# Issuing most output stores from ScalarE's DMA queue in a fused agent-attention and maxout kernel

## The chip, the cores and the metric

The kernel runs on one core of a Trainium2 chip. The metric is the device time of one execution in microseconds (us). The engines are called as in the profile: PE (matrix products; PEld is its loading of weights), ACT (ScalarE), DVE (VectorE), POOL (GpSimd) and SP (SyncE, which here only issues DMAs). A DMA is issued by an instruction on an engine's queue and then carried out by the 16 DMA engines of the core.

## What is computed

Four batches of 12544 rows of 128 numbers go through agent attention with 49 agents, and the result, 50176 rows, through a maxout layer:

```
a2k     = softmax(scale * agents @ k^T)          # per batch, 49 x 12544
agent_v = a2k @ v                                 # 49 x 128
q2a     = softmax(scale * q @ agents^T)           # 12544 x 49
x       = q2a @ agent_v                           # 50176 x 128 over all batches
h       = max(x @ w1, x @ w2, x @ w3)             # 50176 x 768
out     = h @ w_out                               # 50176 x 128
```

All inputs and the output are float32.

## The kernel before

The 50176 output rows are cut into 49 groups of 1024 rows (8 tiles of 128): 48 groups of one batch each, and group 48, which gathers the last two tiles of every batch. A group `s` of this kind is loaded (`ql.s`, L513, SP), cast to bf16 (`qc.s`, L517, POOL), turned either by a DMA transpose (`qd.s`, L454, SP) or on PE (`qt`, `qe`), and scored against the agents (`sc`, `ex`). The two softmaxes are not divided out at once: the weights w1, w2, w3 are multiplied by the agents' values ahead (the G tiles), so that the hidden layer of a group is a product of G with the group's exponentials (`u` and `v`, L558, PE). Maxout is done as relu of a difference and a maximum: for five of the six hidden blocks ACT makes a relu (`a`, L571, tile AS) and DVE takes the maximum (`x`, L574, tile R); for the block 4 ACT does both (L565 and L568). The products with w_out gather in OM (`li`, L582, and `p`, L592, PE), and DVE scales each half of a group's result into the output tile OS (`ov.s.0`, `ov.s.1`, L599). The store `st.s` (L607) sends OS, 512 KB, to the output in DRAM; group 48 is stored in four pieces of 128 KB.

The keys and values of batch 0 are worked through first (to about 45 us). Those of batches 1 to 3 are worked through beside the groups of the batch before: `kl`, `vl` (L325, loads on SP), `kc`, `vc` (L335, casts on POOL), `kt` (L454, DMA transposes on SP), `ks`, `kx`, `kv`, `va` on PE, ACT, PE and DVE, and the sums of exponentials `ea` on POOL (L474).

Two things set the order. The string `ORDER` names every operation in one list that was written ahead from costs and times; each engine runs its own operations in the order of that list, and each operation waits for the data it needs. In the same list the number behind a slash names the buffer that an operation writes. There are three PSUM tiles for the hidden products (UV), two small ones (OM), thirteen load tiles (LD), thirteen R tiles and nine output tiles (OS). All loads, DMA transposes and stores are on SP, so a DMA that waits there holds every later DMA. The only DMA issued elsewhere is the load of the agents at the very start, on ACT.

The layer that builds the program gives every DMA one of eight completion semaphores in turn, in the order of the list and over all issuing engines. A DMA waits, beside its data and its buffer, for the DMA that had its semaphore before, which is the one eight places earlier in the list. ACT's instructions carry one wait themselves; further waits are put into a semaphore instruction ahead.

```
def dma(kb):
    return dict(cost=(0.45, 1.0), serve=kb / 415.0)
...
SLOTS = {"UV": 3, "OM": 2, "LD": 13, ..., "R": 13, "RC": 4, "OS": 9, ...}
...
add(f"st.{s}", SP, em.store(s), after=[f"ov.{s}.0", f"ov.{s}.1"], use=[f"os.{s}"], cost=(0.45, 1.6), serve=524 / 415.0)
```

Of the kernel before, what the change touches and what calls it, by code (L numbers as in the profile page):

```python
# [260 lines left out]
class Emit:  # L261
# [342 lines left out]
    def store(self, s):  # L604
        def fn():
            for cut, r, n in self.rows(s):
                self.nc.sync.dma_start(self.io["out"][r, :].rearrange("(p j) c -> p j c", j=n), self.t[f"os.{s}"][:, cut, :])  # L607
        return fn


# [176 lines left out]
u.35.3/2 v.35.4 a.35.3/2 re.36/0 p.34.0.2 p.34.0.0 li.34.1/0 qd.43/0 qc.40/2 ov.34.0/0 v.35.3/1 x.35.4/8 u.35.1/2 x.35.3/0  # L787
p.34.1.3 p.34.1.5 a.35.1/1 v.35.5/0 p.34.1.4 ql.44/4 x.35.5/2 u.35.2/1 v.35.1/2 a.35.2/2 p.34.1.1 li.35.0/1 p.35.0.3 x.35.1/4
u.35.0/0 v.35.2/1 a.35.0/0 p.35.0.4 p.35.0.5 x.35.2/5 u.36.5/2 p.34.1.0 a.36.5/1 p.34.1.2 u.36.3/0 ov.34.1 v.35.0/1 a.36.3/2
p.35.0.2 x.35.0/6 st.34 u.36.4/2 sc.37/0 ql.42/8 a.36.4 v.36.5/0 qd.40/1 u.36.1/1 x.36.5/7 p.35.0.0 a.36.1/0 p.35.0.1 v.36.4  # L790
ov.35.0/1 v.36.3/0 x.36.4/3 u.36.0/1 x.36.3/9 qc.44/1 li.35.1/1 p.35.1.5 a.36.0/1 v.36.1/2 p.35.1.2 x.36.1/2 u.36.2/0 ex.37/2
v.36.0/1 p.35.1.3 a.36.2/2 p.35.1.4 x.36.0/5 u.37.3/2 su.37/0 p.35.1.0 a.37.3/0 p.35.1.1 u.37.5/0 re.37/2 ov.35.1 v.36.2/1
a.37.5/1 u.37.4/2 qc.42/2 x.36.2/4 li.36.0/0 p.36.0.0 p.36.0.4 a.37.4 p.36.0.5 u.37.1/0 v.37.5/1 a.37.1/2 v.37.4 x.37.5/6 p.36.0.1
# [23 lines left out]
p.42.1.1 p.42.1.0 u.44.4/0 ov.42.1 v.45.2/2 a.44.4 u.44.5/1 x.45.2/4 p.43.0.5 p.43.0.3 p.43.0.4 a.44.5/2 p.43.0.0 su.44/0 v.44.4  # L817
re.44/1 v.44.5/2 ov.43.0/8 x.44.4/8 u.45.1/1 li.43.1/0 x.44.5/5 p.43.1.3 p.43.1.5 a.45.1/0 v.45.0/0 sc.46/1 x.45.0/0 u.44.3/2
ex.46/3 v.45.1/1 p.43.1.4 a.44.3/2 p.43.1.2 x.45.1/7 u.46.0/0 su.45/1 p.43.1.1 a.46.0/1 p.43.1.0 u.46.2/2 re.45/0 ov.43.1 v.44.3/1
a.46.2/0 u.45.4/0 x.44.3/2 st.43 li.44.0/0 p.44.0.5 st.42 p.44.0.0 a.45.4 p.44.0.2 qd.48/0 u.45.5/2 v.46.2/1 a.45.5/2 v.45.4  # L820
x.46.2/3 p.44.0.4 p.44.0.1 st.37 p.44.0.3 x.45.4/10 sc.47/1 ov.44.0/6 v.46.0/2 u.46.1/1 ex.47/2 v.45.5/0 x.46.0/11 li.45.0/0
a.46.1/0 li.44.1/1 p.45.0.0 p.45.0.4 x.45.5/9 u.45.3/2 v.46.1/1 a.45.3/1 p.44.1.5 p.44.1.2 p.44.1.3 x.46.1/5 u.47.0/0 v.45.3/2
a.47.0/2 p.44.1.1 x.45.3/2 u.47.2/1 p.44.1.4 a.47.2/0 p.44.1.0 u.46.4/0 ov.44.1 v.47.2/2 a.46.4 u.46.5/1 x.47.2/6 su.46/1 p.45.0.2
# [40 lines left out]
```

## Time and profile before

| | |
|---|---|
| median of 3 runs | 446.63 us (446.55 to 449.52) |
| the profiled execution | 448.96 us |
| its span, first to last instruction | 447.1 us |
| mean granted TensorE clock | 0.988 |
| busy: PE, DVE, ACT, POOL | 421.8, 392.1, 393.6, 169.5 us |
| DMA traffic | 121.98 MB, 273 GB/s in the mean |
| SP's DMA queue (q1), share of the 16 engines' time | 90.4% |
| stores on SP | 52 issues (48 of 512 KB, 4 of 128 KB), 5.6 us from issue to landing for the large |
| first store issued | 105.4 us after the start |

The profile shows one execution. A page of it gives each engine's busy time, the span in 40 equal slices (each digit is the busy share in tenths), the DMA queues, and the groups of instructions. Views of the trace give more: waits by engine and by what ended them, the timeline of one engine (start, length, line, tile written and read), busy time in chosen stretches, and all instructions that touch a tile or a line. Issuing a DMA is a row of the engine's queue (`SPq`, `ACTq`) and does not count as busy time. The time from issue to landing is the DMA engines' part.

### The profile page before, as it was taken

How to read it: one execution, taken by the hardware profiler on the slowest of the kernel's cores; microseconds unless marked ns; L12 is line 12 of the kernel's file. 1: busy time of each engine (PE TensorE's matmuls, PEld its weight loads, DVE VectorE, ACT ScalarE, POOL GpSimd, SP SyncE). 2: the span in 40 equal slices, each digit the busy share in tenths (PEclk: the TensorE clock that was granted, in tenths of full speed). 3: DMA queues.
4: the chain of work that ended last, by engine and by line, in shares of the span. 5: the costliest groups of instructions: out<-in, count | busy, mean ns of one | idle time of the engine just before them, and what ended most of it. 6: DMA issues, size and time to landing. Idle time of an engine off the chain costs nothing.

```text
span 447.1 us, 12853 instructions
## 1 busy us (share of the span) xinstructions
PE 421.8 (94%) x5260; PEld 270.8 (61%) x5260; DVE 392.1 (88%) x496; ACT 393.6 (88%) x461; POOL 169.5 (38%) x176
## 2 busy tenths in 40 slices
PE   0787899999999999999899999999999999999996
PEld 0554466666666666666566666666665555655675
DVE  1345799999999999999899999998999999999996
ACT  1469799999999999999889999999999999999983
POOL 1641645555694222824871324527601201000000
PEclk9989699999999999999999999999999999999999
DMA  8999999999999999999999999999699464450405
GB/s 312 410 408 387 346 372 281 298 405 308 327 291 307 352 285 285 345 310 225 321 354 253 313 302 345 303 221 353 189 300 282 103 189 122 90 195 22 164 37 202
DMA packets 97045, 121.98 MB, mean 273 GB/s; under 512 B 70423, under 2 KB 73179, under 8 KB 96987
## 3 DMA queue, kind: packets, MB, share of 16 engines
q1 hardware_dynamic: 96784, 121.07, 90.4%
q8 instruction: 41, 0.67, 0.6%
q14 instruction: 17, 0.14, 0.1%
q10 hardware_dynamic: 203, 0.10, 0.1%
HBM read 78.74 MB, written 25.69 MB: 234 GB/s over the span
## 4 chain that ended last, share of the span: by engine, by line
PE 83%; DMA 8%; DVE 3%; issue 2%; POOL 2%; ACT 1%; SPq 1%; DVEq 0%; POOLq 0%
PE UV L558 35%; PE OM L592 31%; PE OM L582 6%; DMA LD<-in_v_dram 4%; PE OM L533 3%; DVE R L574 2%; PE OM L523 2%; DMA LD<-in_k_dram 2%; PE OM L376 2%; PE OM L359 2%; DMA LD<-in_q_dram 1%; PE OM L545 1%; SPq L325 1%; DVE OS L599 1%; POOL QB L517 1%
## 5 line engine op out<-in xcount | busy, mean ns | idle before, releaser
L574 DVE TENSOR_TENSOR R<-UV,AS 128x1024 bf16<-128x1024 f32 x245 | 293.4, 1219 | 17.8 <-PE UV L558 12.9
L571 ACT ACTIVATE AS<-UV 128x1024 bf16<-128x1024 f32 x245 | 246.3, 1024 | 17.8 <-PE UV L558 13.5
L558 PE MATMUL UV<-EQ,G 49*128 49x512 bf16 (+1 forms) x1248 | 181.7, 371 | 0.9
L592 PE MATMUL OM<-wo_bf,R 128*128 128x128 bf16 x2352 | 180.4, 220 | 0.0
L592 PEld LDWEIGHTS <-R 128*128 128x128 bf16 x2352 | 139.8, 98 | 43.4 <-issue 41.1
L558 PEld LDWEIGHTS <-G 49*128 49x128 bf16 x1248 | 61.5, 94 | 61.8 <-issue 21.7
L517 POOL CAST QB<-LD 128x1024 bf16<-128x1024 f32 x49 | 51.1, 1048 | 98.4 <-DMA LD<-in_q_dram 50.3
L335 POOL CAST KB<-LD 128x1152 bf16<-128x1152 f32 (+2 forms) x45 | 49.7, 1116 | 60.4 <-DMA LD<-in_k_dram 42.8
L599 DVE TENSOR_TENSOR OS<-OM,RC 128x512 f32<-128x512 f32 x98 | 67.1, 684 | 3.6 <-PE OM L592 2.5
L335 POOL CAST VB<-LD 128x1152 bf16<-128x1152 f32 (+1 forms) x33 | 37.3, 1137 | 47.7 <-DMA LD<-in_v_dram 14.7
L565 ACT ACTIVATE UV<-UV 128x1024 f32<-128x1024 f32 x49 | 49.8, 1017 | 2.5 <-PE UV L558 1.2
L568 ACT ACTIVATE R<-UV 128x1024 bf16<-128x1024 f32 x49 | 50.1, 1023 | 1.7 <-PE UV L558 1.2
L582 PE MATMUL OM<-G,EQ 128*128 128x256 bf16 x196 | 37.9, 276 | 0.0
L539 ACT ACTIVATE EQ<-OM 128x512 bf16<-128x512 f32 x49 | 29.5, 602 | 0.9 <-PE OM L533 0.6
L474 POOL TENSOR_TENSOR EA<-EA,EK 128x441 f32<-128x441 f32 x27 | 27.6, 1023 | 4.8 <-ACT EK L365 4.1
L347 DVE COPY KT<-UV 128x1152 bf16<-128x1152 bf16 (+1 forms) x12 | 8.2, 700 | 17.3 <-PE UV L342 17.3
L582 PEld LDWEIGHTS <-EQ 128*128 128x128 bf16 x196 | 12.6, 97 | 15.6 <-issue 14.2
L533 PE MATMUL OM<-QT,agT 128*64 128x512 bf16 (+1 forms) x104 | 20.4, 398 | 0.2 <-DMA QT<-QB 0.2
L365 ACT ACTIVATE EK<-OM 128x441 bf16<-128x441 f32 (+1 forms) x33 | 17.8, 540 | 2.9 <-POOL EA L474 1.6
L376 PE MATMUL OM<-EK,VB 128*128 128x49 bf16 x392 | 17.3, 186 | 2.7 <-ACT VB L333 1.4
L359 PEld LDWEIGHTS <-KT 128*128 128x128 bf16 x392 | 14.6, 98 | 7.5 <-issue 4.5
L376 PEld LDWEIGHTS <-VB 128*128 128x128 bf16 x392 | 14.3, 97 | 7.9 <-issue 5.0
(67 smaller groups left out, 186.1 us busy)
## 6 DMA issues: line engine op xcount, KB each, us to landing
LD<-in_q_dram SPq DMA_DIRECT2D x48, 512.0 KB, 6.4
out_dram<-OS SPq DMA_DIRECT2D x48, 512.0 KB, 5.6
LD<-in_k_dram SPq DMA_DIRECT2D x40, 576.0 KB, 7.3
LD<-in_v_dram SPq DMA_DIRECT2D x40, 576.0 KB, 8.7
LD<-in_k_dram SPq DMA_DIRECT2D x3, 512.0 KB, 9.0
LD<-in_v_dram SPq DMA_DIRECT2D x3, 512.0 KB, 8.1
LD<-in_moe_w_dram SPq DMA_DIRECT2D x6, 192.0 KB, 8.4
KT<-KB SPq DMA_TRANSPOSE x33, 7.0
```

What stands on the lines that cost most here:

```text
L335: (self.nc.gpsimd if eng == POOL else self.nc.vector).tensor_copy(out=out, in_=src)
L376: self.nc.tensor.matmul(out, vb[:, j, :], e[:, j * A:(j + 1) * A], start=False, stop=True, skip_group_check=True)
L517: return lambda: self.nc.gpsimd.tensor_copy(out=self.t[f"qb.{s}"], in_=self.t[f"q.{s}"][:, :GT, :])
L533: self.nc.tensor.matmul(self.t[f"qs.{s}"][h * H:(h + 1) * H, jj * P:(jj + pairs) * P], self.agT[:, b, :], self.t[f"qT.{s}"][:, 2 * jj + h: ...
L558: self.nc.tensor.matmul(t[:, h, jj * P:(jj + pairs) * P], self.t[f"G{b}"][h * H:h * H + A, c + f * P:c + (f + 1) * P], self.t[f"e.{s}"][h ...
L565: return lambda: self.nc.scalar.activation(self.t[f"u.{s}.{f}"], self.t[f"u.{s}.{f}"], AF.Relu)
L568: return lambda: self.nc.scalar.activation(self.t[f"r.{s}.{f}"], self.t[f"u.{s}.{f}"], AF.Relu)
L571: return lambda: self.nc.scalar.activation(self.t[f"a.{s}.{f}"], self.t[f"u.{s}.{f}"], AF.Relu)
L574: return lambda: self.nc.vector.tensor_tensor(out=self.t[f"r.{s}.{f}"], in0=self.t[f"v.{s}.{f}"], in1=self.t[f"a.{s}.{f}"], op=ALU.max)
L582: self.nc.tensor.matmul(self.t[f"o.{s}.{o}"][:, i * 2 * C:(i + 1) * 2 * C], self.t[f"e.{s}"][:, jj * P:(jj + 1) * P], self.t[f"G{of[jj]}"] ...
L592: self.nc.tensor.matmul(self.t[f"o.{s}.{o}"][:, c:c + C], self.t[f"r.{s}.{f}"][:, h, jj * P:(jj + 1) * P], self.wo_bf[:, f, :], start=Fals ...
L599: self.nc.vector.tensor_tensor(out=self.t[f"os.{s}"][:, j:j + 4, :], in0=self.t[f"o.{s}.{o}"].rearrange("p (j c) -> p j c", c=C), in1=self ...
```

## The change

The stores of groups 0 to 45 are issued on ACT's queue; those of groups 46, 47 and 48 stay on SP. In the list, the stores keep their places but for two: `st.34` moves behind `u.36.4 sc.37 ql.42 a.36.4`, and `st.43` behind `li.44.0 p.44.0.5 st.42 p.44.0.0 a.45.4`.

```diff
     def store(self, s):
         def fn():
             for cut, r, n in self.rows(s):
-                self.nc.sync.dma_start(self.io["out"][r, :].rearrange("(p j) c -> p j c", j=n), self.t[f"os.{s}"][:, cut, :])
+                (self.nc.scalar if s < 46 else self.nc.sync).dma_start(self.io["out"][r, :].rearrange("(p j) c -> p j c", j=n), self.t[f"os.{s}"][:, cut, :])
         return fn
...
-p.35.0.2 x.35.0/6 st.34 u.36.4/2 sc.37/0 ql.42/8 a.36.4 v.36.5/0 qd.40/1 u.36.1/1 x.36.5/7 p.35.0.0 a.36.1/0 p.35.0.1 v.36.4
+p.35.0.2 x.35.0/6 u.36.4/2 sc.37/0 ql.42/8 a.36.4 st.34 v.36.5/0 qd.40/1 u.36.1/1 x.36.5/7 p.35.0.0 a.36.1/0 p.35.0.1 v.36.4
...
-a.46.2/0 u.45.4/0 x.44.3/2 st.43 li.44.0/0 p.44.0.5 st.42 p.44.0.0 a.45.4 p.44.0.2 qd.48/0 u.45.5/2 v.46.2/1 a.45.5/2 v.45.4
+a.46.2/0 u.45.4/0 x.44.3/2 li.44.0/0 p.44.0.5 st.42 p.44.0.0 a.45.4 st.43 p.44.0.2 qd.48/0 u.45.5/2 v.46.2/1 a.45.5/2 v.45.4
```

## The prediction

> **What bounds the kernel now.** I read the page's slices first, then busy time by stretch, then the waits of each engine, then the DMA issues line by line, and last the timelines of SP and ACT side by side. All times are of the profiled execution: 448.96 us, of which its span is 447.1; it stands 2.3 us above the median of the runs (446.63), so differences are worked out inside it and added to the median.
>
> The slices show three compute engines full from the fourth slice to the last, and the DMA engines full until slice 30 (about 335 us) and then half idle:
>
> ```profile
> PE   0787899999999999999899999999999999999996
> DVE  1345799999999999999899999998999999999996
> ACT  1469799999999999999889999999999999999983
> DMA  8999999999999999999999999999699464450405
> ```
>
> The stretches say how full (columns: length, then busy us and instructions of PE, PEld, DVE, ACT, POOL, then clock, DMA share, GB/s). ACT has 46 to 48 of 50 us, DVE the same:
>
> ```profile
> 150.00:200.00 50.00, 49.88 (x657) 32.56 (x655) 47.77 (x60) 48.18 (x57) 21.67 (x21) 1.00 1.06 309
> 200.00:250.00 50.00, 48.47 (x617) 31.64 (x616) 46.78 (x59) 46.34 (x55) 26.65 (x28) 1.00 1.10 289
> 335.00:400.00 65.00, 64.60 (x667) 36.78 (x665) 61.75 (x68) 61.23 (x69) 9.11 (x9) 1.00 0.58 158
> ```
>
> Who waits for whom (us in total, times, longest): ACT waits in many small pieces for PE's hidden products; SP waits in long ones, 40.6 us of them at the stores; of the compute engines only POOL, 38% busy, waits long for DMAs.
>
> ```profile
> ACT AS L571 <- PE UV L558: 13.5, 38, 1.0
> ACT EK L365 <- POOL EA L474: 1.6, 1, 1.6
> POOL QB L517 <- DMA LD<-in_q_dram: 50.3, 8, 11.9
> SPq L607 <- DVE OS L599: 40.6, 7, 16.1
> ```
>
> So ACT, DVE and PE bound the kernel together. After 50 us all idle time before ACT's instructions is 24.4 us, and the part of it that goes back to a DMA is the one gap of 1.55 us at 216.57. Whatever holds ACT is nearly all lost; whatever helps SP is worth little.
>
> **Gain.** SP loses 46 of its 52 store issues, at a median of 0.52 us some 24 us of SP's time, and its waits for output tiles:
>
> ```profile
> L607 SPq DMA_DIRECT2D out_dram<-OS x52: 332/518/1336, 105.4 to 444.3; - x52
> L454 SPq DMA_TRANSPOSE KT<-KB x33: 1232/3076/9312, 46.5 to 311.8; - x33
> L454 SPq DMA_TRANSPOSE QT<-QB x27: 1232/1645/5177, 132.2 to 414.7; - x27
> ```
>
> (durations in ns, least/median/most). SP is on the chain of waits for 1%, and the DMA pieces there (8%) lie before 42 us, ahead of the first store at 105.4. The bytes stay the same while the DMA engines are full. DVE's wait for a store to free an output tile is 0.3 us in all. The gain is between 0 and 1.55 + 0.3 = 1.9 us; I take 0, since POOL's delay behind that one gap comes from loads whose DMA engines are as full as before.
>
> The Trainium skill, "DMA: Bandwidth & Descriptors", section "Issuing engines are not separate DMA queues", says that moving a DMA to another engine saves only the issuer's time; the shares above bear that out.
>
> **Cost 1, the issue itself on ACT.** The trace has one ACT issue, 0.57 us, for another shape. Bounds for a store: 0.33 us (least on SP) and 1.34 us (most). I take 0.55. Forty-six of them are 25 us if they lie bare, 0 if the queue part of ACT issues while its datapath computes. The trace says the latter: of 340 semaphore instructions on ACT after 50 us the median ends 0.44 us before the ACTIVATE that it guards starts, while the ACTIVATE before it is running (ACT's large ACTIVATEs follow each other at 0.92 us). So an issue has about 0.44 + 0.92 = 1.3 us in which it costs nothing; 0.55 fits, and two in a row (stores 2 and 5, 25 and 27, 44 and 45) just fit. I take 0.4 us in sum, for stores 41 and 39, issued together at 399.4 just as tile 41 becomes ready. If that lead is gone, the cost is the 25 us.
>
> **Cost 2, what ACT now waits for.** In the built order each store still waits for its tile and for the landing of the DMA that stands eight places before it in the program, because eight completion semaphores are handed round over all DMAs. On ACT both waits hold the ACTIVATEs behind them. The tile: ready 3 to 75 us before ACT reaches the store, except stores 23 (0.78 us), 41, 43 and 34 (the two that the order moves later: 1.46 and 1.63); no cost beyond the above. The eighth DMA before: SP lags ACT by up to 8 us between 165 and 270 us, so here the room is thin. Landing against the start of ACT's next instruction: store 9 212.19 against 210.57, store 7 172.94 against 173.13, store 17 246.22 against 246.32, stores 20, 19, 23 and 33 0.3 to 0.9 us ahead, all others over 1.5 us. With 0.6 us for issue and release, store 7 costs 0.4 us and store 9, once ACT is 0.4 late, 1.8 more; then ACT is late enough for the rest. Sum 2.2 us. Behind each stand ACT's relus, for them wait DVE's max, PE's output products and PE's next hidden products (three UV tiles).
>
> **Cost 3, issues that meet a long issue of SP.** While the DMA engines are full, a transpose keeps SP issuing for up to 9.3 us:
>
> ```profile
> 164.93 1.32 SPq L454 DMA_TRANSPOSE QT<-QB  x1
> 166.29 8.02 SPq L454 DMA_TRANSPOSE KT<-KB  x1
> 174.41 1.00 SPq L325 DMA_DIRECT2D LD<-in_v_dram  x2
> 175.46 0.43 SPq L607 DMA_DIRECT2D out_dram<-OS  x1
> ```
> ```profile
> 167.34 3.05 ACT L571 ACTIVATE AS<-UV 128x1024 bf16<-128x1024 f32 x3
> 170.29 1.02 ACT L565 ACTIVATE UV<-UV 128x1024 f32<-128x1024 f32 x1
> ```
>
> Store 6 now stands on ACT before the instruction at 170.29, in the middle of SP's 8.02 us. Nothing in the trace shows an ACT issue beside a transpose. Lower bound: it is not held, 0. Upper bound: it begins when SP's issue ends, as SP's own did at 175.46. Then the delay is the end of SP's row plus 0.6 us minus the start of ACT's next: store 0 (kt1.8 ends 105.34) 2.4, store 1 (113.17) 2.9, store 6 (174.31) 4.6, store 8 (194.27) 3.9, store 13 (209.57) 1.6, store 19 (267.98) 1.6, store 26 (295.52) 1.6, store 37 (416.86) 1.4; together 20.0, with store 9's wait 22.2. The nearest row is the start, where both engines issue at once: ACT's 98 KB take 0.57 us, and SP's first five loads 0.39 to 0.69 us each, where alone they take 0.33. Each slows the other there, so I lean to sharing. But a delay of 3 us shifts ACT against SP, the later meetings change, and ACT's idle time takes some back: I take half, 11 us, and keep 0 and 25 for the range (25: no meeting lost, ACT twice caught behind the same queue).
>
> The Trainium skill, "Perfetto Trace Analysis", section "DMA Instruction — HWDGE (DVE, Sync)", says that an issue locks the descriptor generator for itself until all its descriptors are made. By that rule it would be all 22.2 us, 469 us; no run so far shows it.
>
> **Sum.** 0 gain + 0.4 + 11 (the 2.2 of cost 2 is in it) = 11.4; 446.63 + 11.4 = 458.0 us.
>
> **Rivals.**
> A, not slower: ACT's issue never waits for SP's. Then 0.4 + 2.2 = 2.6 us: 449.2 us, within 1%. For it: SP's plain loads and stores take about 0.5 us even with eight DMAs in flight, so only a transpose fills anything. Against it: the start's rows. It decides if no ACT issue is over 1.4 us.
> B, the eighth-DMA wait becomes the bound: a store now passes SP's loads that would have gone first. SP's landings follow each other at 1.43 us (165.67, 167.09, 168.52), so each passed load lands that much later; the seven stores with under 1 us of room would cost 1.4 us more each at worst, of which ACT's own lateness spares about half: 2.6 + 5 = 7.6, 454 us.
> C, SP's freedom helps: loads and transposes go out earlier, the gap at 216.57 and DVE's 0.3 us go: 444.7 us. More would need idle time on ACT, DVE or PE that a DMA ends, and there is none.
> That the stores would not move is excluded: the built order has 46 more DMAs on ACT.
>
> **How the numbers follow.** Forecast (issues held, 452 to 472) 0.43; A (446 to 451) 0.40; B (451 to 456) 0.12; C 0.05, of which 0.03 for more than I can see. A measurement of this kernel can tell about 1% (4.5 us) from no change: slower 0.43 + 0.12 = 0.55, same 0.40 + 0.02 = 0.42, faster 0.03. The forecast's own range is 452 to 472, with both ends of cost 3; the range that holds 8 in 10 must take in A, so 446 to 472.
>
> **What would show it.** Cost 1: ACT's stores at 0.4 to 0.6 us with no gap behind most of them; wrong if every store has a gap of its length, 25 us. Cost 2: ACT gaps that end with a DMA landing, near stores 7 and 9. Cost 3: ACT issues of 2 to 9 us that end with a transpose's issue, with gaps of the same length in ACT's, then DVE's rows between 100 and 335 us, and none after 335; wrong if ACT's longest store issue is under 1.4 us. Gain: SP's waits for output tiles gone while POOL still waits for loads. The prediction as a whole is wrong if ACT's idle time after 50 us grows by less than 5 us.

## The result and the profile after

The change makes the kernel slower: 475.54 us (median of 4 runs, 472.66 to 478.80) against 446.63 us (446.55 to 449.52) beside it. The ratio is 1.0633, with a 95% interval of 1.0552 to 1.0714. The prediction was 458.0 us, in a range of 446 to 472; the sign is right, the time lies above the range. The profiled execution took 472.66 us with a span of 470.8, 23.7 us more than the 447.1 before. Some executions of a kernel took over 1.5% longer than its fastest: the ratios below leave them out, and where the profiled execution was one of them (e5_head with 485.3 us, e7_but3 with 474.3 us) its rows are read for the places of the gaps, with their lengths as no more than a hint.

The slices of the changed kernel answer to those shown of before, and the clock's row stands with them:

```profile
PE   0778999997999996799999899999987999989996
DVE  1346999996999996699999899988975999989996
ACT  1468999995989995799989899998865999989983
PEclk9998999998999999799999999999997999999999
DMA  8999999999999999999999999999796353252405
```

The engines are as busy as before (ACT 393.7 us against 393.6, DVE 394.2 against 392.1), but their rows have holes in common: in the 10th slice (106 to 118 us), the 16th and 17th (177 to 200) and the 30th and 31st (341 to 365). The busy time by stretch says the same (columns as in the prediction): of the 48.18 us that ACT worked between 150 and 200 us, 40.55 are left, and of 61.23 between 335 and 400 us, 53.25.

```profile
150.00:200.00 50.00, 43.53 (x542) 27.88 (x539) 40.57 (x51) 40.55 (x48) 20.60 (x20) 0.93 1.06 300
200.00:250.00 50.00, 49.43 (x629) 32.03 (x626) 47.98 (x60) 47.20 (x56) 25.75 (x28) 1.00 1.08 286
335.00:400.00 65.00, 58.72 (x610) 33.67 (x606) 54.37 (x62) 53.25 (x61) 9.38 (x9) 0.95 0.65 175
```

The waits name who is late (us in total, times, longest):

```profile
DVE R L574 <- PE UV L558: 26.5, 41, 6.0
PE UV L558 <- ACT AS L571: 15.5, 10, 5.7
ACT AS L571 <- PE UV L558: 14.5, 38, 1.5
ACT AS L571 <- DMA LD<-in_v_dram: 6.2, 1, 6.2
ACT AS L571 <- DMA LD<-in_q_dram: 5.3, 1, 5.3
ACT AS L571 <- DMA LD<-in_k_dram: 2.8, 1, 2.8
ACT EK L365 <- PE OM L359: 2.3, 1, 2.3
```

ACT's relu of the hidden layer (tile AS) uses no load of v, q or k; still it waits 6.2, 5.3 and 2.8 us for one. None of these three rows was there before, nor the second row, in which PE waits for ACT. SP, meanwhile, waits less for output tiles (40.6 us before; what is left are the stores that stay):

```profile
SPq L607 <- DVE OS L599: 29.9, 3, 21.9
```

ACT's idle time after 50 us grew from 24.4 to 48.6 us, by 24.2, which is about the growth of the span. The three rows are the time that ACT's queue stood at a store. The longest, in ACT's timeline of the changed kernel (start, length, line, tile, in brackets the idle time before):

```profile
182.49 1.02 ACT L565 ACTIVATE UV<-UV 128x1024 f32<-128x1024 f32 x1
189.26 0.34 ACTq L607 DMA_DIRECT2D out_dram<-OS  x1
189.71 1.02 ACT L571 ACTIVATE AS<-UV 128x1024 bf16<-128x1024 f32 x1 [6.19 <-DMA LD<-in_v_dram]
```

This is store 12. Its tile had been ready since 165 us. Its issue takes 0.34 us, but begins at 189.26, and 0.02 us earlier, at 189.24, the load `vl2.10` landed, which had the same completion semaphore. Of the 46 stores 14 begin within 0.1 us after the landing of the DMA that had their semaphore before.

The time of the issues themselves (durations in ns: least, median, most):

```profile
L607 ACTq DMA_DIRECT2D out_dram<-OS x46: 338/339/1582, 101.0 to 457.9; - x46
L607 SPq DMA_DIRECT2D out_dram<-OS x6: 333/376/440, 457.8 to 468.0; - x6
```

The holes can also be read as lag. The table gives how much later DVE starts the same maximum (L574) than in the kernel before, by the time of that instruction before; a step is where time is lost, and a constant value is where nothing happens. The names are those of the experiments below.

| time before (us) | 106 | 116 | 176 | 186 | 246 | 256 | 334 | 344 | 396 | 405 | 440 |
|---|---|---|---|---|---|---|---|---|---|---|---|
| changed kernel | -2.0 | 3.0 | 3.5 | 11.3 | 10.2 | 12.0 | 14.9 | 21.8 | 22.0 | 23.7 | 23.7 |
| e2_touch | -0.8 | 4.8 | 6.6 | 14.4 | 13.3 | 13.6 | 13.7 | 19.6 | 19.6 | 19.6 | 19.6 |
| e3_touch_const | -0.7 | -0.7 | 0.5 | 0.6 | -0.3 | 0.1 | 0.2 | 0.2 | 0.2 | 0.2 | 0.2 |
| e1_pool | -1.5 | -1.2 | 4.6 | 4.6 | 9.0 | 9.0 | 10.4 | 10.4 | 10.6 | 10.6 | 10.6 |
| e4_tail | -1.6 | -1.6 | 0.1 | 0.1 | 1.4 | 1.4 | 1.4 | 1.4 | 1.4 | 2.7 | 2.7 |
| e9_tail_spread | -1.3 | -1.0 | 0.5 | 0.5 | -0.3 | -0.3 | -0.3 | -0.3 | -0.3 | 0.1 | 0.1 |
| e7_but3 | 1.0 | 5.1 | 10.3 | 11.8 | 10.5 | 13.7 | 24.1 | 24.1 | 24.1 | 25.4 | 25.4 |
| e8_free | -0.8 | 4.6 | 4.5 | 4.5 | 6.0 | 6.0 | 7.3 | 7.3 | 7.3 | 8.6 | 8.6 |
| e10_st0 | -0.5 | 2.2 | 2.7 | 2.7 | 3.2 | 3.2 | 3.2 | 3.2 | 3.2 | 3.2 | 3.2 |
| e13_best | -1.2 | -1.2 | -1.3 | -1.3 | 0.2 | 0.2 | 0.4 | 0.4 | 0.4 | 0.9 | 0.9 |

Three steps, of 5.1, 7.8 and 6.9 us, make up 19.8 of the changed kernel's 23.7 us. Small steps say little: e4_tail is the kernel before up to 344 us, in the order of its DMAs too, and still its lag goes from -1.6 to 1.4 us by then, in steps of up to 1.7 us. A step of that size is read below only where the timeline shows its gap.

### The profile page after: what moved, and what is told of

Same layout as the page of the kernel before. It is cut to its first block, busy times and chain, and to the rows that moved or that the text cites. A ratio compares the mean times of both kernels' runs of the same rounds, so it can differ in the third digit from the quotient of the medians.

```text
span 470.8 us, 12849 instructions
## 1 busy us (share of the span) xinstructions
PE 426.1 (91%) x5260; PEld 271.8 (58%) x5260; DVE 394.2 (84%) x496; ACT 393.7 (84%) x461; POOL 169.7 (36%) x176
## 5 line engine op out<-in xcount | busy, mean ns | idle before, releaser
L574 DVE TENSOR_TENSOR R<-UV,AS 128x1024 bf16<-128x1024 f32 x245 | 294.1, 1220 | 36.8 <-PE UV L558 26.5
L558 PE MATMUL UV<-EQ,G 49*128 49x512 bf16 (+1 forms) x1248 | 184.1, 372 | 18.9 <-ACT AS L571 15.5
L517 POOL CAST QB<-LD 128x1024 bf16<-128x1024 f32 x49 | 50.8, 1042 | 105.0 <-DMA LD<-in_q_dram 44.2
L582 PE MATMUL OM<-G,EQ 128*128 128x256 bf16 x196 | 38.2, 277 | 0.4 <-ACT EQ L539 0.3
L365 ACT ACTIVATE EK<-OM 128x441 bf16<-128x441 f32 (+1 forms) x33 | 17.9, 541 | 4.9 <-PE OM L359 2.3
L582 PEld LDWEIGHTS <-EQ 128*128 128x128 bf16 x196 | 12.8, 98 | 15.6 <-issue 14.1
L359 PEld LDWEIGHTS <-KT 128*128 128x128 bf16 x392 | 14.5, 98 | 9.9 <-issue 4.2
```

What stands on the lines that cost most here:

```text
L517: return lambda: self.nc.gpsimd.tensor_copy(out=self.t[f"qb.{s}"], in_=self.t[f"q.{s}"][:, :GT, :])
L558: self.nc.tensor.matmul(t[:, h, jj * P:(jj + pairs) * P], self.t[f"G{b}"][h * H:h * H + A, c + f * P:c + (f + 1) * P], self.t[f"e.{s}"][h ...
L574: return lambda: self.nc.vector.tensor_tensor(out=self.t[f"r.{s}.{f}"], in0=self.t[f"v.{s}.{f}"], in1=self.t[f"a.{s}.{f}"], op=ALU.max)
L582: self.nc.tensor.matmul(self.t[f"o.{s}.{o}"][:, i * 2 * C:(i + 1) * 2 * C], self.t[f"e.{s}"][:, jj * P:(jj + 1) * P], self.t[f"G{of[jj]}"] ...
```

## The experiments

The leading theory (waiting): a store on ACT waits for a recent load or transpose of SP that had its semaphore, and holds every ACTIVATE behind it. The rivals: traffic (stores on a second queue make loads and transposes late) and issue (46 issues cost ACT their own time). The times of before beside the runs were 448.3 to 448.7 us; ratios are to these.

**Is it ACT that is held, or the traffic? Stores on GpSimd's queue.**

```diff
-                (self.nc.scalar if s < 46 else self.nc.sync).dma_start(
+                (self.nc.gpsimd if s < 46 else self.nc.sync).dma_start(
```

> The same 46 stores leave SP as in the changed kernel, at the same places of the list, but GpSimd's queue issues them; ACT issues none. Waiting theory (ACT itself is held because a store on it waits for a recent load of SP that used the same completion semaphore): ACT is free again, 444 to 452 us. Traffic theory (stores on a second queue go ahead of loads and make the loads, transposes and casts late): the stores are on a second queue here too, so 465 us or more. Issue theory (46 issues cost ACT their own time): as the waiting theory, so this run only parts the traffic theory from the other two. POOL may itself be held by the stores; if its casts come late, ACT's gaps end with POOL's or a DMA's work and the time lies between.

Measured: 460.21 us, ratio 1.0223 (1.0163 to 1.0282). No theory had this: of the loss of 6.3%, 2.2% is left. After the first 50 us ACT has no gap that a DMA ends. The stores on POOL took turns on eight semaphores of their own, so none of them waited for a load. What is left comes from DVE, which now waits for stores to free an output tile. In the kernel before and with the stores on POOL:

```profile
DVE OS L599 <- DMA out_dram<-OS: 0.3, 1, 0.3
```
```profile
DVE OS L599 <- DMA out_dram<-OS: 7.1, 3, 3.2
```

The three waits (2.73 us before 135.12, 3.23 before 196.69, 1.16 before 338.65) stand where this run's lag grows, by 5.7 us between 126 and 137 us, by 4.3 near 190 and by 1.3 ahead of 334. Behind the first, PE's L582 waits 2.81 us for DVE, and ACT's exponentials of keys (L365) start 2.85 us late; behind the second it is 2.92 and 2.55 us. The stores that ended these two waits were issued by POOL at 125.97 and 188.01 us and landed 9.1 and 8.6 us later. So with ACT free of stores its long gaps are gone, and the loss that stays is another one, of stores that come late on POOL's queue. Whether POOL got to them too late (it is 24 us busier with the issues) or they landed slowly is not separated. This run speaks neither for the traffic theory nor against it; the runs with store 0 below test it.

**The waits alone, with no DMA on ACT.** `tw.s` stands behind `st.s` in the list at 22 of the places:

```diff
+    def touch(self, tile):
+        return lambda: self.nc.scalar.activation(self.touched, self.t[tile][:, 0, :1], AF.Copy)
...
+TOUCH = {0: 'v2.3', 1: 'k2.6', 5: 'q.13', 3: 'k2.3', 4: 'k2.7', 11: 'q.17', 7: 'v2.7', 12: 'v2.10', 8: 'q.21', ...}
```

> The kernel before, all stores on SP, and 22 added ACTIVATEs of 128x1 at the places where stores stand in ACT's order in the changed kernel; each reads a tile that the load or transpose brings for which the store there waits in the changed kernel. So the waits are on ACT, but no DMA is. (The added instructions write a tile that nothing reads.) Waiting theory: most of the loss of 29 us comes back, 462 to 476 us, with ACT gaps of several us in front of the added instructions. Traffic theory and issue theory: no DMA moves, so 447 to 452 us, the added instructions' own time of some 0.2 us each.

The control reads a constant at the same places (`self.ident[:, :1]` in place of the tile):

> Control for the run with 22 added ACTIVATEs: the same instructions at the same places, but they read a constant that is there from the start, so they wait for nothing. Every theory: 447 to 452 us (22 times some 0.2 us). If it is as slow as the run that reads loaded tiles, that run shows nothing of waiting.

Measured: 465.33 us, ratio 1.037 (1.0315 to 1.0426), against 449.25 us, ratio 1.001 (0.9982 to 1.0038), for the control. The waits alone cost 16.1 us, and the table shows the three steps at the same places, of 5.5, 7.8 and 5.9 us. The timeline of the run with waits, at the place of store 12:

```profile
185.55 1.02 ACT L571 ACTIVATE UV<-UV 128x1024 f32<-128x1024 f32 x1
191.06 0.20 ACT L611 ACTIVATE touched<-LD 128x1 f32<-128x1 f32 x1 [4.50 <-DMA LD<-in_v_dram]
191.17 1.01 ACT L577 ACTIVATE AS<-UV 128x1024 bf16<-128x1024 f32 x1
```

An instruction of 0.20 us stands 4.50 us at the place where the store stood 6.19, for the same load. So the waiting theory carries more than half of the loss of 28.9 us. The 10 us between the medians of this run and of the changed kernel must come from something else; between the two profiled executions (468.51 and 472.66 us) it is 4.1 us.

**The two ends of the kernel.** Stores 34 to 45 alone on ACT, and stores 0 to 33 alone:

```diff
-                (self.nc.scalar if s < 46 else self.nc.sync).dma_start(
+                (self.nc.scalar if 34 <= s < 46 else self.nc.sync).dma_start(    # e4_tail
+                (self.nc.scalar if s < 34 else self.nc.sync).dma_start(          # e5_head
```

> Only stores 34 to 45 go to ACT's queue, where the DMA that had the same completion semaphore is old and landed long before; stores 0 to 33 stay on SP. Waiting theory: 446 to 452 us; the few us are stores issued one right behind the other. Issue theory: 12 of 46 issues, so about a quarter of the loss, 452 to 456 us. Traffic theory: the DMA engines are half idle there, 446 to 449 us.

> The other part of the run that moves stores 34 to 45: here stores 0 to 33 go to ACT's queue and the rest stay on SP. Waiting theory: all the large waits are here (behind the loads and transposes of the last few us), so 470 to 475 us, 1.4 us less than the changed kernel or so, with the three large jumps at the same places (near 114, 189 and 355 us). Issue theory: 34 of 46 issues, 466 to 468 us.

Measured: 450.21 us, ratio 1.0031 (1.0000 to 1.0061), for the tail; ratio 1.0600 (1.0543 to 1.0657) for the head, 475.3 us on 448.36. The tail's twelve issues cost 1.4 us (0 to 2.7) and the head's thirty-four the rest: it is not a price per issue. The head's longest gaps stand at the same places as the changed kernel's, at store 12 (7.9 us) and at store 33 (6.3 us).

**Issues in a row.** What the tail does lose, it loses at one place: its timeline shows three issues that take 2.57 us together, and a gap.

```profile
397.48 1.02 ACT L571 ACTIVATE AS<-UV 128x1024 bf16<-128x1024 f32 x1
397.49 2.57 ACTq L607 DMA_DIRECT2D out_dram<-OS  x3
400.15 1.94 ACT L571 ACTIVATE AS<-UV 128x1024 bf16<-128x1024 f32 x2 [1.65 <-PE UV L558]
```

The edit moves each of five stores behind a later ACTIVATE:

```diff
-... a.42.3/2 v.43.1/1 ... st.35 qd.45/1 st.40 st.36 u.44.2/0 a.44.2/0 ... a.44.0/1 ...
+... a.42.3/2 st.35 v.43.1/1 ... qd.45/1 u.44.2/0 a.44.2/0 st.40 ... a.44.0/1 st.36 ...
```

> Stores 34 to 45 on ACT, as in the earlier run, but stores 35, 40, 36, 39 and 45 moved by one or two of ACT's instructions in the list, so that none is issued right behind another. If a second store in a row takes over 1 us because the queue still holds the first, the gap of 1.65 us near 400 us goes, the four issues take 0.34 us each, and the time is 446 to 449 us, some 1.3 us under the run without this. If the length of an issue has to do with its place and not with the one before, nothing changes: 449 to 451 us.

Measured: 449.16 us, ratio 1.0024 (0.9996 to 1.0051). The gap at 400 us is gone and with it the step of 1.3 us in the table; by their ratios alone the two runs can't be told apart. The cause given in the expectation holds only in part: ten of the twelve issues took 0.34 to 0.40 us, two still took 1.13 and 1.19, and they cost no gap. In the changed kernel the issues at 335.6 (1.58 us), 337.3 (1.14), 418.4 (1.28) and 419.8 (1.25), each close behind others, go with gaps of 1.2 us at 337 and 2.0 us at 421.

**Without the three longest waits.**

```diff
+                (self.nc.scalar if s < 46 and s not in (1, 12, 33) else self.nc.sync).dma_start(
```

> The changed kernel, but stores 1, 12 and 33, in front of whose places ACT stood longest (2.8, 6.2 and 5.3 us), stay on SP: 43 stores on ACT in place of 46. Waiting theory: the three gaps go, 20 us of lag with them at most; other stores then wait instead, since ACT is no longer late when it reaches them: 451 to 462 us. Issue theory and traffic theory: 43/46 of the loss, 471 to 475 us.

Measured: ratio 1.0394 (1.0289 to 1.0499), 466.0 us on 448.36. This lies between the two ranges: 4 us over the waiting theory's and 5 us under the others'. The three gaps are gone, and others are in their place:

```profile
ACT AS L571 <- DMA LD<-in_q_dram: 6.2, 1, 6.2
ACT EQ L539 <- DMA QT<-QB: 5.0, 1, 5.0
```

The first is store 24, behind the load `ql.34`, where ACT had 0.8 us in the changed kernel. There `ql.34` was issued 9.9 us later than in the kernel before, here 14.3 us later, about as late as ACT itself. This fits the waiting theory: a store that ACT reaches late, because it stood elsewhere, finds its DMA landed, and one that it reaches in time waits. The second is store 7, with 0.7 us in the changed kernel, and it has another cause: with three stores back on SP the semaphores fall out differently, and its predecessor is the transpose `qd.17` in place of the load `vl2.7`. So a few stores taken back do not give back their share.

**Only stores with an old predecessor.**

```diff
+                (self.nc.scalar if s in (0, 2, 5, 10, 11, 16, 25, 27, 28, 29, 31) or 34 <= s < 46 else self.nc.sync).dma_start(
```

> 23 stores on ACT, half of the 46: 0, 2, 5, 10, 11, 16, 25, 27, 28, 29, 31 and 34 to 45. They are chosen so that in the built program the DMA which had the same semaphore landed 1.5 us or more before ACT reaches the store, by the times of the kernel before. Waiting theory: 447 to 452 us, and what is left of the loss stands where stores are issued one right behind the other (25, 27, 29, 31 near 330 us, 36 and 40 near 400 us, about 1.3 us each). Issue theory and traffic theory: half of the loss, 456 to 462 us.

Measured: 457.27 us, ratio 1.0192 (1.0139 to 1.0244). The waiting theory alone is wrong here, by 5 us. The table shows where: two steps of 1.3 us near 330 and 400 us, at issues in a row, as expected, but also 5.4 us between 106 and 116 us, where the only store on ACT is store 0, and ACT stands only 0.7 us at it. It then waits for PE's scores of keys (L365 <- L359, 2.66 us at 110.9), and these wait 2.4 us for a key transpose.

**Store 0 alone.** It is on ACT at its place (first), on ACT three of its instructions later (second), and on SP between the two key transposes of that time (third):

```diff
+                (self.nc.scalar if s == 0 else self.nc.sync).dma_start(      # e10_st0, e11_st0_late
...
-... x.6.0/4 li.6.0/1 st.0 a.7.5/0 ... vl1.9/3 ex.8/2
+... x.6.0/4 li.6.0/1 a.7.5/0 ... vl1.9/3 ex.8/2 st.0                         # e11_st0_late
-... qc.10/2 kt1.8/0 ... st.0 ...
+... qc.10/2 st.0 kt1.8/0 ...                                                 # e12_st0_between
```

> The kernel before, with store 0 alone on ACT's queue, at its place. Overtaking theory (a store on a second queue moves its data beside a transpose already issued and makes it land late): the transpose for the keys issued just before lands 10.9 us after its issue instead of 6.7 to 8.2, the exponentials of the keys (L365) start 2.3 to 2.7 us late, and the run loses 4 to 5 us: 450 to 453 us. Waiting theory alone: ACT waits for a load that lands as it gets there, 0 to 0.7 us: 446 to 449 us.

> Store 0 alone on ACT's queue again, but some three of ACT's instructions later in the list, where SP has ended the issue of both key transposes. Overtaking theory: the transposes land 8 to 10 us after their issue, and the time is 446 to 449 us. If it is the second queue as such, and not the meeting with the transposes, it stays at 450 to 453 us.

> No store on ACT. Store 0 stays on SP, but stands in front of the second of the two key transposes, so it is issued about when ACT issued it. If a store on the same queue keeps its turn behind the first transpose, that one lands 7 to 9 us after its issue and the second up to 2 us later than before: 446 to 450 us. If any store at this time makes the first transpose land 10.9 us after its issue, whichever queue it is on: 450 to 453 us.

Measured: 451.60 us, ratio 1.0048 (1.0017 to 1.0080); 448.81 us, 1.0014 (0.9988 to 1.0040); 448.28 us, 0.9997 (0.9976 to 1.0018). The DMA rows of the stretch from 99 to 101.5 us, in which the first of the two transposes is issued (last column: us from issue to landing), in the kernel before, where store 0 is issued on SP behind both:

```profile
KT<-KB SPq DMA_TRANSPOSE x1, 6.7
```

for store 0 on ACT at its place:

```profile
KT<-KB SPq DMA_TRANSPOSE x1, 10.9
```

for store 0 on ACT a little later:

```profile
KT<-KB SPq DMA_TRANSPOSE x1, 8.2
```

and for store 0 on SP, behind that transpose:

```profile
KT<-KB SPq DMA_TRANSPOSE x1, 8.1
```

In the third run the store is issued at 103.18 us, 4.0 us after the transpose began to issue, in the first at 102.90, 3.2 us after, in the second at 106.94, 6.0 us after. So on SP's queue the store kept its turn; on ACT's queue, at nearly the same time, it shared the DMA engines at once, and the transpose that was first landed 2.7 us later. The exponentials of the keys then start 2.52 us late in the first run (with no gap in the two others), and the run loses 2.6 us there, where 4 to 5 were expected. The Trainium skill, "DMA: Bandwidth & Descriptors", section "Queues, rings and completion order", says that a DMA engine takes turns between the queues that have work for it; these three rows agree.

In the changed kernel this is not one case only. From 100 to 335 us the groups of transposes have medians from issue to landing of, before,

```profile
KT<-KB SPq DMA_TRANSPOSE x26, 7.1
QT<-QB SPq DMA_TRANSPOSE x17, 7.1
```

and, after,

```profile
KT<-KB SPq DMA_TRANSPOSE x26, 8.2
QT<-QB SPq DMA_TRANSPOSE x15, 9.1
```

Transposes that took over 10 us were 4 of 43 before, 16 of the same 43 after, and 11 with the stores on POOL. So the traffic theory is right as the smaller part: it explains store 0's step, and the late DMAs add to the waits of other stores. By how much can be read at the three longest. In the profile of before the DMAs that stores 12, 1 and 33 wait for landed 4.6, 2.6 and 5.2 us after the start of ACT's next instruction; the gaps in the changed kernel are 6.2, 2.8 and 5.3 us. So at store 12 some 1.6 us are added, at the other two next to nothing. How much of the 10 us that the waits alone leave open is due to it, and how much to issues in a row, was not separated further.

**All three causes avoided.** The stores of the run with 23, without store 0, and with the issues in a row spread:

```diff
+                (self.nc.scalar if s in (2, 5, 10, 11, 16, 25, 27, 28, 29, 31) or 34 <= s < 46 else self.nc.sync).dma_start(
...
-... st.27 ks3.10/0 p.32.1.5 st.25 ... kx3.10/3 st.31 v.33.2/1 a.34.5/2 st.29 ... a.33.0/1 to3
+... st.27 ks3.10/0 p.32.1.5 ... kx3.10/3 st.25 v.33.2/1 a.34.5/2 st.31 ... a.33.0/1 st.29 to3
```

> 22 stores on ACT: those of the run with 23, without store 0, and with stores 25, 27, 29, 31 and 35, 36, 39, 40, 45 moved by one or two of ACT's instructions so that none is issued right behind another. If the three costs found (waiting for a recent load, overtaking a transpose, two issues in a row) are all there is, 446 to 450 us, the kernel before or a little over it, with ACT's idle time after 60 us at 24 to 27 us. Issue theory or traffic theory in general: 456 us or more.

Measured: 450.52 us, ratio 1.0042 (1.0011 to 1.0074). This is half a microsecond over the expected range. ACT's idle time after 50 us is 25.4 us, against 24.4 before. Not all issues in a row are gone: four still took 1.06 to 1.23 us. Twenty-two issues on ACT cost 0.4% when none waits or overtakes and few follow closely. They gain nothing either: no version with stores on ACT was faster than the kernel before.

## Why the prediction was wrong

**The step that failed: Cost 2, "the landing of the DMA that stands eight places before it in the program".** The rule is right: a store on ACT waits for the DMA eight places before it. But the places were counted in the written list, and the semaphores are handed round in the order of the built program. In the kernel before the two are the same for all 262 DMAs, which is why the description above takes them for one; with stores on ACT they are not: store 0 comes in the built program after the loads `kl2.2` and `kl2.6`, which follow it in the list. Counted in the list, the real predecessor of a store on ACT stands 3 to 10 places before it (median 6), so it is mostly a younger DMA. For store 12 it is `vl2.10`, 3 places before. The prediction's figure for store 9 shows the slip: 212.19 us is the landing of `kt2.9`, eight places before in the list, but the semaphore was that of `qd.21`, which landed at 212.97. With the right names, the landings of the profile of before would have shown it: 17 of the 46 stores have their predecessor land 0.3 us or more after ACT's next instruction starts, up to 5.8 us (store 20), store 12 by 4.6. The prediction had 2.2 us, for stores 7 and 9. The three waits that the profile after names sum to 14.3 us, and the waits alone cost 16.1 us in the run made for them.

**Cost 3, issues held by SP's long issues, was wrong, and with it the forecast's 11 us.** It was to show as ACT issues of 2 to 9 us that end with a transpose's issue. SP's timeline and ACT's, in the changed kernel, at stores 3 and 4:

```profile
148.45 7.96 SPq L454 DMA_TRANSPOSE KT<-KB  x1
```
```profile
149.21 0.34 ACTq L607 DMA_DIRECT2D out_dram<-OS  x1
150.74 0.34 ACTq L607 DMA_DIRECT2D out_dram<-OS  x1
```

Both take the median 0.34 us inside a transpose's issue of 7.96 us, and of the 25 ACT issues that overlap a transpose's issue 24 took under 0.7 us. The Trainium skill's rule in "Perfetto Trace Analysis", section "DMA Instruction — HWDGE (DVE, Sync)", that an issue locks the descriptor generator until its descriptors are made, does not hold across these two engines here; the measurement decides. The few long issues (up to 1.58 us, over the 1.4 us that the prediction named as its mark) follow other stores on ACT and do not end with a transpose. So the 11 us of the forecast stood on a mechanism that these runs do not show, and that its sign came out right is luck as far as it rested on them.

**Cost 1 was right in the mean.** The issue is 0.34 us where 0.55 was taken, and it hides behind the ACTIVATE before it; the tail run's price is 1.4 us for twelve. The estimate of 0.4 us missed that some issues close behind others take 1.1 to 1.6 us; why is open.

**The gain was right: none.** SP waits less for output tiles and has the issues no more, and POOL waits for loads nearly as long as before (QB for the q loads 44.2 us, before 50.3). The two moves in the list cost nothing: the runs of the tail contain both, and their lag is constant from 334 to 396 us, around the first, and from 405 to 440 us, around the second.

**The rivals.** A said that ACT's issues never wait for SP's, 449 us: its mark, no issue over 1.4 us, is missed by little (1.58 us, and for another reason), and its time fails by the same Cost 2 that it contained. B named both mechanisms that the runs show, a wait on the eighth DMA and a store that passes SP's loads, and put them at 7.6 us and a chance of 0.12. Its price took the seven stores with little room from the wrong list, and it took ACT's lateness to spare half. Store 24 in the run without three stores fits such a sparing; but there SP's load came as late as ACT's work did, and a new wait stood later. C expected a gain, and there was none.

**The test that held** was the last one: ACT's idle time after 50 us grew by 24.2 us, well over the 5 us named.

## What to carry to other kernels

Before a DMA is moved to a compute engine's queue, look up in the built program which DMA its semaphore had before, and compare that landing with the time at which the engine gets there; a wait on a compute engine holds all its work behind it, while on SP it held only other DMAs. A second queue also takes a DMA out of its turn: what was issued earlier on the other queue, and is needed sooner, can land later (10.9 us after its issue here, in place of 8.1). Another engine's queue has costs of its own: on POOL the stores came too late to free their tiles. The issue itself is the smallest part.

## What the runs showed of the hardware that was not expected

A long pause of ACT cost more than its length: PE pauses with it (from 183 to 190 us it worked 2.07 of 7.00 us) and comes back at half clock. The stretches of the changed kernel around stores 12 and 33 (the number behind POOL's column is the granted clock):

```profile
190.00:194.00 4.00, 3.22 (x29) 2.01 (x28) 2.35 (x2) 3.16 (x4) 3.92 (x4) 0.50 0.99 355
194.00:198.00 4.00, 4.00 (x56) 2.65 (x55) 3.00 (x5) 3.70 (x5) 3.42 (x5) 0.97 1.14 328
355.00:359.00 4.00, 2.69 (x18) 1.43 (x19) 1.75 (x2) 2.86 (x3) 0.49 (x1) 0.50 1.10 329
359.00:363.00 4.00, 4.00 (x32) 2.02 (x32) 2.84 (x3) 2.16 (x3) 1.04 (x1) 0.69 0.31 122
```

Gaps of 6.19 and 5.29 us became steps of 7.8 and 6.9 us, some 1.6 us more each. Behind store 33 the timeline shows it, as two waits of ACT for PE, 1.46 and 1.22 us; behind store 12 it rests on the lag alone. The Trainium skill, "TensorE: Matmul & The Clock Gate", section "What's actually happening", says that the clock is halved after an idle window of some 3.4 us; these rows agree.

An ACT issue of a 512 KB store took 0.34 us in the median, also while SP was issuing, where SP's own took 0.52 us before the change.
